# A pad of 160 bytes for 32 at the right end of SBUF, in a transformer block on one core

## The chip, the core and the metric

The kernel runs on one core of a Trainium2 chip. The time is that of the device for one execution, in microseconds. Before the change it is 955.4 us, the median of three runs (954.83 to 955.71).

The engines are called as in the profile: PE (TensorE, with PEld for its weight loads), DVE (VectorE), ACT (ScalarE), POOL (GpSimd), and SP, whose queue issues nearly all DMAs.

## The reference: what is computed

One transformer block over S = 2048 tokens of D = 512, in float32, with adaptive layer norms, sliding-window attention (32 heads of 16, window 256) and a SwiGLU feed-forward part (F = 1792):

```python
mod = (_silu(c) @ w_mod).reshape(c.shape[0], 6, 1, -1)
sa, ca, ga, sb, cb, gb = (mod[:, 0], mod[:, 1], mod[:, 2], mod[:, 3], mod[:, 4], mod[:, 5])
h = _layernorm(x, axis=-1) * (1 + ca) + sa
x = x + ga * _A_ref(h, A_wqkv, A_wo)        # qkv, masked softmax per head, output projection
h = _layernorm(x, axis=-1) * (1 + cb) + sb
x = x + gb * _B_ref(h, B_w1, B_w3, B_w2)    # (silu(h w1) * (h w3)) w2
```

## The kernel before, in words

**Precision.** Most products are made of two-part numbers: an operand is cut into a high part (an ACT copy to fp32r) and a low part (the rest, by DVE or POOL), and a product is three matmuls, high by high, high by low, low by high. One such matmul has a weight tile of 128x128, loaded before it, and a moving operand of 128x512. Every matmul loads other weights than the one ahead of it, so PE's rows alternate: a weight load, a matmul, a weight load, a matmul. In the trace the load for the next matmul starts a few ns after the current matmul does, so that the two read SBUF side by side.

**Stages.**
- Ahead of about 100 us: layer norm, the values' projection (`value`, L705: weights are 128-column slices of `hT`, the moving operand is `wvh` or `wvl`), and the first query and key projections.
- About 100 to 470 us, attention, in 32 units (8 groups of 4 heads by 4 blocks of tokens): the projection of queries and keys (`product`, L520: weights `wq`, moving `hT`), scores for the row maxima (L576) and for the probabilities (L933), both with weights and moving operand from the tile `ring` and moving 384 columns in the main, and the product with the values (L894: weights `vS`, moving `pt`).
- About 470 to 520 us: the output projection (`o_proj`, L1317: weights `o` or `x1b`, moving `wo`).
- From about 520 us: the feed-forward part, 14 rounds (2 halves of the tokens by 7 pairs of columns of F). In each round `ffn` makes the gate and the up product, each as 7 block products of 6 matmuls (`product`, L1581: weights `w` or, in every second round, `wo` and `o`; moving `b`). The results are combined on DVE, POOL and ACT, cut into two parts, and multiplied down (`down`, L1675: 8 blocks of 6 matmuls; weights are the slices of the cut results, moving `w2`).

The names `wo` and `o` stand for two things: the output projection's weights and inputs, and later the feed-forward weights of every second round (`second_open` puts those into the same places). The cut results of a round lie in `wq00`, `wq10`, `wq01`, `wq11`, `qkr`, `qk0`, `qk1`, `qk2`; in the last round four of the eight are `e0`, `e1`, `e2` and `wqr` instead.

**Order.** The order of instructions on every engine comes from a planner in the kernel with costs and offsets written out as tables. It knows nothing of addresses.

**Places in SBUF.** Pools are stacked from both ends of each partition's 224 KB: `cst`, `ap`, `p0`, `a2`, `fp` from the left, and `edge`, `a1`, `hp` (later `xp`) from the right. `edge` is the first pool on the right and holds one tile that nothing reads or writes. Everything on the right lies below it, so its size sets where all of them start:

```python
ctx.enter_context(tc.tile_pool(name="edge", bufs=1, side="right")).tile([P, 8], F32, name="edge")
a1 = ctx.enter_context(tc.tile_pool(name="a1", bufs=1, side="right", reuse_waits="tile"))
...
hp = hx.enter_context(tc.tile_pool(name="hp", bufs=1, side="right", reuse_waits="tile"))
hT = hp.tile([P, 2, KC, S], F32R, name="hT")
```

The start of the larger tiles in a partition, as the built programs have it, in bytes modulo 512 (a weight slice of 128 columns is 512 bytes, so all slices of a tile start at the same place modulo 512; a moving operand of 512 columns is 2048 bytes):

| side | tiles | before | after |
|---|---|---|---|
| left | `ring`, `vS`, `mskq`; feed-forward: `b`, `w` (all four tiles), `w2`, `t`, `g`, `e` | 448 | 448 |
| left | `wvh`, `wvl`; `pt`, `sm`, `jb`, `os` | 64 | 64 |
| left | `xt`, `h32` | 416 | 416 |
| right | `hT`; `x1a`, `x1b`, `wo`, `o`; `qkr`, `qk0`, `qk1`, `qk2`, `wqr`, `wq00`, `wq01`, `wq10`, `wq11` | 64 | 448 |
| right | `junk` (two buffers) | 128, 384 | 0, 256 |

Of the kernel before, what the change touches and what calls it, by code (L numbers as in the profile page):

```python
# [8 lines left out]
F32 = mybir.dt.float32  # L9
# [9 lines left out]
P = 128  # L19
# [349 lines left out]
def block_kernel(ctx: ExitStack, tc: tile.TileContext, x, wqk, wv, wo, w13, w2, c, crow, wmod, wmodt, out):  # L369
# [40 lines left out]

    psA = ctx.enter_context(tc.tile_pool(name="psA", bufs=1, space=PSUM))

    ctx.enter_context(tc.tile_pool(name="edge", bufs=1, side="right")).tile([P, 8], F32, name="edge")
    a1 = ctx.enter_context(tc.tile_pool(name="a1", bufs=1, side="right", reuse_waits="tile"))

    def ps(b):
# [1395 lines left out]
```

## Time and profile before

| | |
|---|---|
| median of 3 runs | 955.4 us (954.83 to 955.71) |
| the profiled execution | 954.43 us, of which its span from the first to the last instruction is 952.7 us |
| PE | 936.7 us busy (98%), 5296 matmuls |
| DVE / ACT / POOL | 734.2 (77%) / 560.8 (59%) / 497.6 us (52%) |
| granted TensorE clock, mean | 0.998 |
| DMA | 141.64 MB, 149 GB/s mean |
| chain that ended last | PE 86%, POOL 4%, DVE 4%, DMA 2%, ACT 2% |

A matmul's duration in the trace reaches to the modelled end of its pipeline, so consecutive matmuls overlap and durations can't be added up. The pace of PE is read from starts: in the chain that ended last, each piece runs from its start to the start of the next.

### The profile page before, as it was taken

The numbers are of one execution on the slowest core, as the hardware profiler recorded it, in microseconds if no ns is written. First come the engines' busy times: TensorE is split into PE (matmuls) and PEld (weight loads), VectorE is DVE, ScalarE is ACT, GpSimd is POOL, SyncE is SP. The second block draws the span as 40 slices with busy tenths as digits, with TensorE's granted clock in tenths as the row PEclk, the third lists the DMA queues.
The fourth block names the chain that finished last, engine by engine and source line by source line (L and its number), as shares of the span: only waits on it lengthen the run. The fifth ranks groups of instructions, "written<-read, shape, count | busy, mean of one in ns | idle before, by whom it ended". The sixth has DMA issues, their size and how long they took to land.

```text
span 952.7 us, 17091 instructions
## 1 busy us (share of the span) xinstructions
PE 936.7 (98%) x5296; PEld 715.5 (75%) x5296; DVE 734.2 (77%) x2065; ACT 560.8 (59%) x1263; POOL 497.6 (52%) x721
## 2 busy tenths in 40 slices
PE   8999999999999999998999999999999999999998
PEld 4678777777767677775688888888888888888886
DVE  7884989898989898989469775666689766667555
ACT  6443878787878787876779933433456333433230
POOL 3220877787777777767544655444866222221320
PEclk9999999999999999999999999999999999999999
DMA  8621454444544444436993555466684421322002
GB/s 310 209 68 37 127 185 146 147 146 147 160 166 146 146 147 146 136 129 207 261 275 100 175 160 200 136 187 215 223 287 144 149 79 60 99 83 78 23 23 88
DMA packets 81561, 141.64 MB, mean 149 GB/s; under 512 B 10555, under 2 KB 23227, under 8 KB 81470
## 3 DMA queue, kind: packets, MB, share of 16 engines
q1 hardware_dynamic: 81180, 140.29, 45.8%
q8 instruction: 42, 0.69, 0.3%
q14 instruction: 49, 0.40, 0.1%
q10 hardware_dynamic: 290, 0.27, 0.1%
HBM read 85.73 MB, written 34.61 MB: 126 GB/s over the span
## 4 chain that ended last, share of the span: by engine, by line
PE 86%; POOL 4%; DVE 4%; DMA 2%; ACT 2%; issue 2%; SPq 1%; POOLq 0%; DVEq 0%; ACTq 0%
PE st L1581 12%; PE mx L1581 10%; PE pj L520 8%; PE mx L576 7%; PE st L933 7%; PE mx L1675 7%; PE po L894 7%; PE st L1675 5%; PE pj L1581 3%; PE po L1581 3%; PE mx L705 2%; PE po L1675 2%; PE st L1317 2%; PE pj L1675 2%; PE mx L1317 2%; PE st L705 2%
## 5 line engine op out<-in xcount | busy, mean ns | idle before, releaser
L583 DVE CUSTOM_DVE_ANT_0 junk<-mx,mskq 128x384 bf16<-128x384 f32 (+1 forms) x482 | 242.1, 528 | 24.6 <-PE mx L576 23.2
L576 PE MATMUL mx<-ring 96*128 96x384 f32 (+2 forms) x482 | 144.8, 340 | 2.2 <-ACT pt L945 1.0
L933 PE MATMUL st<-ring 100*128 100x384 f32 (+2 forms) x484 | 145.7, 342 | 0.7 <-ACT pt L954 0.4
L961 POOL TENSOR_SCALAR_AFFINE_SELECT pt<-pt 128x256 f32<-128x256 f32 x268 | 108.1, 406 | 50.2 <-ACT pt L954 39.7
L520 PE MATMUL pj<-hT,wq 128*128 128x512 f32 x384 | 132.0, 403 | 0.0
L954 ACT ACTIVATE pt<-st 128x256 f32<-128x256 f32 x255 | 91.3, 386 | 36.1 <-DVE st L951 28.2
L576 PEld LDWEIGHTS mx<-ring 96*128 96x128 f32 x482 | 88.0, 189 | 31.5 <-DVE mt L583 21.1
L933 PEld LDWEIGHTS st<-ring 100*128 100x128 f32 x484 | 89.9, 189 | 18.9 <-issue 6.7
L1625 POOL TENSOR_TENSOR t<-t,t 128x512 f32<-128x512 f32 x28 | 41.6, 1485 | 113.8 <-DVE t L1613 106.7
L894 PE MATMUL po<-pt,vS 128*17 128x256 f32 (+2 forms) x1408 | 97.1, 387 | 2.4 <-ACT os L1001 1.0
L538 POOL TENSOR_TENSOR qk<-qkr,qk 128x512 fp32r<-128x512 f32 x64 | 82.8, 1293 | 10.2 <-ACT qkr L526 8.7
L1172 POOL TENSOR_TENSOR w<-w,w 128x512 fp32r<-128x512 f32 (+2 forms) x35 | 51.4, 1480 | 58.7 <-ACT w L1171 58.7
L1613 DVE TENSOR_TENSOR t<-st,t 128x512 f32<-128x512 f32 x55 | 37.8, 690 | 50.8 <-PE st L1581 38.3
L520 PEld LDWEIGHTS pj<-hT,wq 128*128 128x128 f32 x384 | 71.2, 189 | 7.5 <-issue 0.9
L951 DVE COPY_PREDICATED st<-later,st 128x128 f32<-128x128 uint8 x255 | 68.8, 291 | 7.6 <-PE st L933 4.4
L894 PEld LDWEIGHTS po<-pt,vS 128*17 128x17 f32 x1408 | 32.1, 96 | 48.4 <-issue 19.6
L1581 PE MATMUL st<-b,w 128*128 128x512 f32 x234 | 58.9, 390 | 0.0
L945 ACT ACTIVATE pt<-st 128x384 f32<-128x384 f32 (+2 forms) x113 | 47.0, 432 | 14.9 <-DVE st L941 13.7
L978 POOL TENSOR_SCALAR_AFFINE_SELECT sm<-sm 128x256 f32<-128x256 f32 x109 | 41.9, 406 | 24.2 <-ACT sm L968 21.4
L1581 PE MATMUL mx<-b,w 128*128 128x512 f32 x204 | 51.5, 390 | 0.0
L1581 PEld LDWEIGHTS st<-b,w 128*128 128x128 f32 x234 | 43.9, 188 | 9.3
L1653 ACT ACTIVATE qkr<-g 128x512 fp32r<-128x512 f32 x13 | 8.2, 632 | 66.5 <-DVE g L1609 66.5
(349 smaller groups left out, 2140.3 us busy)
## 6 DMA issues: line engine op xcount, KB each, us to landing
ring<-qk SPq DMA_DIRECT2D x192, 128.0 KB
o_dr<-os SPq DMA_DIRECT2D x32, 256.0 KB
w<-wsum SPq DMA_DIRECT2D x14, 512.0 KB
w<-w2g SPq DMA_DIRECT2D x14, 512.0 KB
jb<-in_w SPq DMA_DIRECT2D x24, 256.0 KB
vS<-in_wmodt SPq DMA_DIRECT2D x22, 256.0 KB
wraw<-in_w SPq DMA_DIRECT2D x7, 768.0 KB
w<-wraw SPq DMA_DIRECT2D x14, 384.0 KB
```

The source lines that it names most:

```text
L520: nc.tensor.matmul(v["ps"], WQ[g][w][:, n // 3], hTp(i, n // 3, b * BT, BT), start=(n == 0), stop=(n == 3 * KC - 1))
L538: nc.gpsimd.tensor_tensor(out=v[n], in0=v["raw"], in1=v[1].bitcast(F32), op=ALU.subtract)
L576: nc.tensor.matmul(v[i][:, :n], queries(NS, a, gq, 1), keys(NS, hh, a, k0, gq + 1 - k0), start=True, stop=True)
L583: nc.vector.tensor_tensor_reduce(out=junk[:, :n], in0=v[i][:, :n], in1=mskq[:, 3 * P - n:], scale=1.0, scalar=-3e38, op0=ALU.add, op1=ALU. ...
L894: nc.tensor.matmul(po[32 * i:32 * i + DH + 1, qb * P:(qb + nq) * P], vS[:, kb, 4 * g + i], pts[i // 2][:, i % 2, c0:c0 + nq], start=first, ...
L933: nc.tensor.matmul(ps[:, :nq], keys(NM, hh, a, kb, 1), queries(NM, a, kb, nq), start=True, stop=not plus)
L951: nc.vector.copy_predicated(ps[:, 0], later, ps[:, 2])
L954: nc.scalar.activation(pt_of(j, a)[:, hh, :2], v[j, a, hh][:, :2], AF.Exp, scale=SCALE)
L961: nc.gpsimd.affine_select(out=pt[:, :, 2 * m], in_=pt[:, :, 0], **w)
L1172: sch.op(eng, lambda: on_eng(eng).tensor_tensor(out=lo(), in0=src(), in1=hi().bitcast(F32), op=ALU.subtract), tt(eng, n), key, kl + kh, kl ...
L1581: nc.tensor.matmul(ps(bk), WT[s, n][w][:, col], BB[t, k][r], start=start and c == 0, stop=stop and c == 5, skip_group_check=True)
L1675: nc.tensor.matmul(ps(bk), tiles[hk + (h,)][:, i * P:(i + 1) * P], w2_of(last, y, f), start=(m == 0), stop=(m == 5))
```

## The change

The tile of the pool `edge` has 40 floats per partition where it had 8, that is 160 bytes for 32. Every tile on the right side moves down by 128 bytes. The left side stays. No instruction is added or removed, and on every engine the instructions stand in the same order with the same waits; only addresses of right-hand operands differ.

```diff
     psA = ctx.enter_context(tc.tile_pool(name="psA", bufs=1, space=PSUM))
 
-    ctx.enter_context(tc.tile_pool(name="edge", bufs=1, side="right")).tile([P, 8], F32, name="edge")
+    ctx.enter_context(tc.tile_pool(name="edge", bufs=1, side="right")).tile([P, 40], F32, name="edge")
     a1 = ctx.enter_context(tc.tile_pool(name="a1", bufs=1, side="right", reuse_waits="tile"))
```

## The prediction

> **What bounds the kernel now.** The page comes first: its busy times, and the chain that ended last by engine.
>
> ```profile
> span 952.7 us, 17091 instructions
> PE 936.7 (98%) x5296; PEld 715.5 (75%) x5296; DVE 734.2 (77%) x2065; ACT 560.8 (59%) x1263; POOL 497.6 (52%) x721
> PE 86%; POOL 4%; DVE 4%; DMA 2%; ACT 2%; issue 2%; SPq 1%; POOLq 0%; DVEq 0%; ACTq 0%
> ```
>
> PE carries the chain. The change touches no instruction, so it can act only where an address sets how long something takes. The place to look is PE's pace, and the second view is the chain in order of time inside the feed-forward part (start, length until the next piece starts, piece). I took 655 to 720 us, since there whole rounds of both kinds stand side by side.
>
> ```profile
> 662.86 2.79 PE mx L1581 x12
> ...
> 678.20 2.78 PE mx L1675 x12
> 680.98 2.79 PE st L1675 x12
> 683.77 1.40 PE pj L1581 x6
> ...
> 694.90 1.36 PE pj L1581 x6
> ...
> 707.14 1.36 PE st L1581 x6
> 708.50 1.37 PE mx L1581 x6
> ```
>
> Two paces are in it. From 662.86 to 678.20 stand 66 matmuls in 15.34 us, 232.4 ns each. From 678.20 to 683.77 stand 24 in 5.57 us, 232.1 ns each. From 694.90 to 708.50 stand 60 in 13.60 us, 226.7 ns each. The form is the same (128x128 weights, 512 columns). The third view, PE's timeline of the same stretch, says what differs:
>
> ```profile
> 662.69 2.96 PE L1581 MATMUL mx<-b,wo 128*128 128x512 f32 x12
> 678.50 1.09 PE L1675 MATMUL mx<-w,qk 128*128 128x512 f32 x4
> 694.74 1.52 PE L1581 MATMUL pj<-b,w 128*128 128x512 f32 x6
> ```
>
> In the slow rows the moving operand lies on the left at byte 448 modulo 512 (`b`, `w2`) and the weights on the right at 64 (`wo`, `o`, `qkr`, `qk`, `wq`). In the fast row both lie at 448. The stages view of exactly these two stretches keeps other causes out:
>
> ```profile
> 662.86:678.20 15.34, 15.34 (x67) 1.00 0.69 226
> 694.90:708.50 13.60, 13.60 (x61) 1.00 0.74 246
> ```
>
> PE is busy throughout both, the granted clock (behind the count) is 1.00 in both, and the DMA share is higher in the fast one. So neither waits, nor the clock, nor DMA traffic makes the slow pace.
>
> Is it the distance modulo 512, or that the weights are on the right? Two other stages tell. Their pieces of the chain, and two groups that name their operands (shortest, median and longest duration behind the count):
>
> ```profile
> 86.87 4.12 PE st L705 x18
> 91.00 2.04 PE mx L705 x9
> ```
>
> ```profile
> 475.34 2.72 PE mx L1317 x12
> 482.82 4.08 PE mx L1317 x18
> ```
>
> ```profile
> L705 PE MATMUL mx<-wvh,hT x72: 388/389/500, 21.4 to 92.6; 128*128 128x512 f32 x72
> L1317 PE MATMUL mx<-wo,o x48: 389/389/396, 475.2 to 518.5; 128*128 128x512 f32 x48
> ```
>
> In the values' projection (L705) the moving `wvh` is on the left and the weights, slices of `hT`, are on the right, both at 64: 2.04 us for 9 is 226.7 ns. In the output projection (L1317) both are on the right at 64: 4.08 us for 18 is 226.7 ns again. So right-hand weights run at the fast pace, with a moving operand from the left too, wherever both stand at the same byte modulo 512. I read the extra 5.7 ns (232.4 less 226.7) as the price of reading a moving operand and the next weights at different bytes modulo 512.
>
> The Trainium skill, in TensorE: Matmul & The Clock Gate, section "Step-by-step: what each phase is for", says that PE has two independent read ports and that loading the next weights takes no read bandwidth from the running matmul. By that rule alone the change would be worth nothing; the trace disagrees, with 232.4 against 226.7 ns for one form.
>
> **The change part by part.** *Feed-forward part.* After the change the right side is at 448 as well, so every pair of moving operand and weights in it meets at the same byte. How many matmuls are slow now: 7 of the 14 rounds have their gate and up weights in `wo` and `o`, each with 2 times 7 products of 6 matmuls, which is 588. The down products are 14 times 8 blocks of 6, 672, with right-hand weights in all but 20 (in the last round, for the second half of its blocks, five of six matmuls use `e0` to `e2`). That is 652. Together 1240 times 5.7 ns is 7.1 us.
>
> Do they lie on the path? In the stages view PE is busy for all of 530 to 930 us:
>
> ```profile
> 530.00:930.00 400.00, 400.00 (x1750) 1.00 0.43 137
> ```
>
> What would be late next if PE goes faster: a slow round (84 matmuls at L1581, 48 at L1675) becomes shorter by 0.75 us of some 30, the others by about 0.27. The engines that feed and empty PE wait there themselves (waits from 530 to 950 us: total, times, longest):
>
> ```profile
> POOL w L1172 <- ACT w L1171: 57.9, 14, 14.3
> DVE t L1613 <- PE st L1581: 38.3, 34, 2.1
> ```
>
> DVE waits for PE's results and POOL has up to 14 us to spare in cutting weights, so I count nothing back; if this cover were thin, I allow up to 2 us lost over the 14 rounds. The term is 7.1 us less, between 5.0 and 8.2 less (the upper end takes the slowest of the quoted pieces, 1.40 us for 6, which is 233.3 ns and 6.6 over the fast pace).
>
> *Values' projection.* `hT` moves to 448 and `wvh`, `wvl` stay at 64, so its 192 matmuls lose their match: at 5.7 ns, 1.1 us more. How much is on the path, by the chain's shares of the first 100 us:
>
> ```profile
> by line: PE mx L705 22.9%; PE st L705 14.9%; PE pj L520 8.8%; PE po L766 6.0%; DVE vS L723 5.8%; PE st L732 3.8%; PE st L576 3.1%; DVE hT L699 3.1%; PE st L685 3.1%; PE mx L576 2.7%; PE mx L685 2.7%; PE mx L732 2.7%; issue 2.4%; DVE xt L676
> ```
>
> 37.8 us of the 43.5 (192 times 226.7 ns) are on it, so the bound is 0.95 us. The distance here is 384 bytes where the feed-forward part has 128, and no fast-form row shows 384 by itself; the lower bound is nothing. I take 0.8 us more, nearer to the row that shows a price.
>
> *Attention.* Here `hT` and `wq` (64, later 448) alternate with `ring` (448), so matches are gained: behind a projection step the next weights are often of `ring`, and the other way round. But the timeline shows little to gain:
>
> ```profile
> 65.33 2.01 PE L520 MATMUL pj<-hT,wq 128*128 128x512 f32 x8
> 67.18 0.34 PE L576 MATMUL st<-ring 96*128 96x384 f32 x1
> ...
> 265.43 0.86 PE L520 MATMUL pj<-hT,wq 128*128 128x512 f32 x3
> 266.13 0.34 PE L933 MATMUL st<-ring 100*128 100x384 f32 x1
> 266.31 0.34 PE L576 MATMUL mx<-ring 96*128 96x384 f32 x1
> 266.48 0.34 PE L933 MATMUL st<-ring 100*128 100x384 f32 x1
> 266.66 0.40 PE L520 MATMUL pj<-hT,wq 128*128 128x512 f32 x1
> 266.90 0.34 PE L933 MATMUL st<-ring 100*128 100x384 f32 x1
> ```
>
> Three projection steps in a row (both operands at 64) take 0.70 us, 233 ns each, and one with `ring` behind it 240 ns; eight in a row take 1.85 us, 231 ns. Scores followed by scores take 0.17 to 0.18 us, scores followed by a projection 0.18 us. So in this mix even the matched steps are slow. Perhaps a mismatch is felt for a step or two, and in runs this short the fast pace is never reached; after the change the runs of matched steps become longer. The bound: 384 projection steps and 848 score steps of 384 columns, in these groups,
>
> ```profile
> L933 PE MATMUL st<-ring 100*128 100x384 f32 x424 | 132.7, 352 | 0.7 <-ACT pt L954 0.4 <-ACT pt L945 0.2
> L520 PE MATMUL pj<-hT,wq 128*128 128x512 f32 x384 | 132.0, 403 | 0.0
> L576 PE MATMUL mx<-ring 96*128 96x384 f32 x424 | 131.3, 349 | 2.2 <-ACT pt L945 1.0 <-DVE st L951 0.7 <-ACT pt L954 0.4
> ```
>
> each 2 ns faster (233 to 231, the step of the longest run), is 2.5 us less. A loss is possible too where `pt` (64) now meets `wq` at 448, but that is one step per unit, under 0.2 us over 32 units. I take 0.5 us less, nearer to the rows in which match and mismatch read alike.
>
> *Other engines.* DVE, ACT, POOL and the DMA queues get new addresses as well. In the feed-forward rounds the work of ACT, DVE and POOL already goes both from left to left (448 to 448) and from left to right (448 to 64), without a wait that PE's rows would show; I cost it at nothing.
>
> **The sum.** 7.1 less, 0.8 more, 0.5 less: 6.8 us less. The span goes from 952.7 to 945.9 us. The profiled execution took 954.43 us, 1.73 more than its span, so it would be 947.6; the median of the runs, 955.4, is 1.0 above that execution, which gives 948.6 us.
>
> **The rivals.**
>
> *No match is needed; right-hand weights are slow for another reason (the same time, 955.4 us).* All slow rows of the feed-forward part do have their weights on the right. Against it stand L705 and L1317, with right-hand weights at 226.7 ns. Chance 0.05.
>
> *The match at 448 is paid for elsewhere.* Once the right side stands at 448 too, ACT and DVE write the cut results there while PE reads at 448, and half of the steps might stay slow: 3.5 us less in place of 7.1, hence 952.2 us. Against it: in the fast rounds PE reads at 448 while `t` and `g` at 448 are read and written, at 226.7 ns. Chance 0.05.
>
> *A denser PE loses clock (slower).* The feed-forward part is 420 us of PE without a break. If the faster pace drew a lower granted clock there, each per cent would cost 4.2 us; from 1.7% on the gain is gone, and at 3% the time is 955.4 less 6.8 plus 12.6, 961.2 us. For it: the matmul array would work 2.5% more densely in the slow stretches. Against it: the granted clock reads 1.00 in 13.6 us at the fast pace and over 530 to 930 us, which holds both. Chance 0.04.
>
> **How the numbers follow.** The forecast has 0.86, with 948.6 us. Its low end is 8.2 and 2.5 less, nothing lost in the values' projection, and 0.5 for the spread of the runs: 944.2, which I draw in to 945.0, since these ends are unlikely together. Its high end is 5.0 less, 0.95 more, and nothing gained in attention: 951.4, drawn in to 951.2 for the same reason. The rivals lie outside, with 0.14. A measurement of this kernel can tell about 0.2%, 1.9 us, from no change. Faster by more than that are the forecast and the second rival, 0.91; within it the first, 0.05; slower the third, 0.04.
>
> **What would show it.** Right: the chain after shows 1.36 us for 6 at L1581 and L1675 in every round, whatever the operands; the feed-forward part, from the first L1581 to the last L1675, is about 7 us shorter; L705 pieces of 9 take 2.09 us in place of 2.04. Wrong: rows with `b,wo` or `w,qk` still at 1.40 us for 6 (the first rival), both kinds at some 1.38 (the second), a granted clock below 0.99 between 530 and 930 us (the third), or an attention stage that moves by more than 2.5 us.

## The result, and the profile after

The changed kernel takes 947.3 us, the median of four runs (946.36 to 948.02), against 955.1 us before (four runs, 953.89 to 955.71): a ratio of 0.992, 95% interval 0.990 to 0.994. The profiled execution took 948.02 us, its span is 946.3 us.

The page after, span and busy times:

```profile
span 946.3 us, 17091 instructions
PE 930.7 (98%) x5296; PEld 716.4 (76%) x5296; DVE 736.4 (78%) x2065; ACT 560.1 (59%) x1263; POOL 498.0 (53%) x721
```

PE is busy 6.0 us less with the same 5296 matmuls; DVE, ACT and POOL work as long as before, to within 2.2 us. The chain in order of time, in the stretch where the prediction read two paces:

```profile
661.93 2.72 PE mx L1581 x12
664.65 2.72 PE st L1581 x12
...
676.89 2.72 PE mx L1675 x12
679.61 2.72 PE st L1675 x12
682.33 1.36 PE pj L1581 x6
...
693.21 1.36 PE pj L1581 x6
```

One pace is left: 1.36 us for 6, in rounds with `wo` and `o`, in rounds with `w`, and in the down products. The 66 steps of the round with `wo` and `o`, from its first piece to the first down product, take 14.96 us where they took 15.34, 226.7 ns each. The stages view of 530 to 900 us says the same by counting, before and then after (length, PE busy and matmuls, PEld, DVE, ACT and POOL likewise, granted clock, DMA):

```profile
530.00:900.00 370.00, 370.00 (x1621) 302.22 (x1620) 256.50 (x336) 159.39 (x251) 159.95 (x145) 1.00 0.46 147
```

```profile
530.00:900.00 370.00, 370.00 (x1651) 306.87 (x1650) 262.22 (x344) 160.29 (x253) 160.59 (x145) 1.00 0.45 147
```

PE is busy without a break in both, at clock 1.00, and gets through 30 matmuls more. The length of the whole feed-forward part is read from the start of its first matmul to the start of its last one (the first and the last start of a group stand behind its durations), before and then after:

```profile
L1581 PE MATMUL st<-b,w x234: 388/389/396, 513.3 to 903.5; 128*128 128x512 f32 x117
L1675 PE MATMUL mx<-w,wq x144: 390/393/404, 561.3 to 948.1; 128*128 128x512 f32 x144
```

```profile
L1581 PE MATMUL st<-b,w x234: 388/389/397, 514.6 to 898.2; 128*128 128x512 f32 x117
L1675 PE MATMUL mx<-w,wq x144: 388/389/389, 562.1 to 941.7; 128*128 128x512 f32 x144
```

From 513.3 to 948.1 it was 434.8 us, from 514.6 to 941.7 it is 427.1: 7.7 us less. It begins 1.3 us later, however. The product with the values marks attention, before and after:

```profile
L894 PE MATMUL po<-pt,vS x1408: 271/379/499, 98.8 to 470.5; 128*17 128x384 f32 x64, 128*17 128x256 f32 x56, 128*17 128x128 f32 x56
```

```profile
L894 PE MATMUL po<-pt,vS x1408: 271/379/847, 99.2 to 471.8; 128*17 128x384 f32 x64, 128*17 128x256 f32 x56, 128*17 128x128 f32 x56
```

0.4 us were lost ahead of attention and 0.9 in it (371.7 us before, 372.6 after). The loss in attention goes with a lower clock, not with the change: in this execution the granted clock fell to 0.70 from 445 to 450 us and to 0.62 from 450 to 455 us, behind a wait for the DMA that brings `wo` from `wog` (439.27 us, 6.49 us long), and the stages view has a mean of 0.93 around it. In the changed kernel's second profile (below) the clock stayed at 1.00 there, and attention took 371.9. Four of the kernels below whose addresses in attention are those of before show such a fall too. Why it comes in some executions is not known; the kernel before has the same wait, 6.38 us, at a clock of 1.00.

```profile
430.00:480.00 50.00, 46.10 (x321) 0.93 0.77 229
```

### The profile page after: what moved, and what is told of

It is laid out like the page before. It is cut to its first block, busy times and chain, and to the rows that moved or that the text cites. A ratio compares the mean times of both kernels' runs of the same rounds, so it can differ in the third digit from the quotient of the medians.

```text
span 946.3 us, 17091 instructions
## 1 busy us (share of the span) xinstructions
PE 930.7 (98%) x5296; PEld 716.4 (76%) x5296; DVE 736.4 (78%) x2065; ACT 560.1 (59%) x1263; POOL 498.0 (53%) x721
## 4 chain that ended last, share of the span: by engine, by line
PE 86%; DVE 4%; POOL 4%; ACT 2%; DMA 2%; issue 2%; SPq 0%; POOLq 0%; DVEq 0%; ACTq 0%
PE st L1581 12%; PE mx L1581 10%; PE pj L520 8%; PE mx L576 7%; PE st L933 7%; PE po L894 7%; PE mx L1675 7%; PE st L1675 5%; PE pj L1581 3%; PE po L1581 3%; PE po L1675 2%; PE mx L705 2%; PE st L1317 2%; PE pj L1675 2%; PE mx L1317 2%
```

## The experiments

Theory 1 says that a matmul step is slow where moving operand and weights stand at different bytes modulo 512. Theory 2 says that it is the place or the side: that the right side is better off at 448 than at 64. All pads below hold nothing and move only what lies behind them.

**The changed kernel again** is the measure for the three that follow, on the same chip, with the kernel before at 954.1 us. The later ones ran on other chips, each with the kernel before beside it, so their ratios are what to compare.

> The changed kernel once more, beside the kernel before on the same chip, as the measure for the others. 0.992 of the kernel before (947.3 where that is 955.1), with 1.36 us for 6 matmuls at L1581 and L1675 in every round and 2.10 us for 9 at L705.

It took 947.2 us, ratio 0.993 (0.992 to 0.994).

**A pad on the left instead of the right.**

```diff
             pools["fp"] = fp
+            fp.tile([P, 32], F32, name="fedge")
```

> The pad on the right stays at 32 bytes; instead the pool fp on the left begins with 128 unused bytes, so that in the feed-forward part both sides meet at byte 64. Theory 1 (what counts is that moving operand and weights stand at the same byte modulo 512, wherever that is): all of L1581 and L1675 at 1.36 us for 6, 7.1 to 7.7 us less; L705 stays at 2.04 us for 9 and attention as before, so 947.5 us or, without the 0.8 us that the values' projection cost in the changed kernel, down to 946.5. Theory 2 (the right side is better off at 448 than at 64): no change, 955.1.

946.6 us, ratio 0.992 (0.991 to 0.994). The chain, in the feed-forward part and at the end of the values' projection:

```profile
662.39 2.72 PE mx L1582 x12
...
677.35 2.72 PE mx L1676 x12
...
693.67 1.36 PE pj L1582 x6
```

```profile
84.57 2.04 PE mx L705 x9
```

Every row is fast although the right side stands at 64 as before. Theory 2 has fallen: it is not the side and not the place, but where the two operands stand to each other.

**The values' projection matched as well.** In the changed kernel the small tiles of `p0` go first, with 32 bytes behind them, so that `wvh` and `wvl` come to 448.

```diff
+    mv = p0.tile([P, NT, 2], F32, name="mv")
+    rs = p0.tile([P, NB, 2, 4], F32, name="rs")
+    bst = p0.tile([P, 4, nc.vector.BN_STATS_DIM], F32, name="bst")
+    p0.tile([P, 8], F32, name="pedge")
     crep = p0.tile([P, D], F32, name="crep")
 ...
-    mv = p0.tile([P, NT, 2], F32, name="mv")
-    rs = p0.tile([P, NB, 2, 4], F32, name="rs")
-    bst = p0.tile([P, 4, nc.vector.BN_STATS_DIM], F32, name="bst")
```

> The changed kernel, with the small tiles of the pool p0 ahead of crep, wvh and wvl and 32 unused bytes behind them, so that wvh and wvl stand at 448 as hT does. Theory 1: L705 back at 2.04 us for 9, 0.8 to 1.0 us less than the changed kernel, 946.4; if attention gains from hT and wq standing at 448 as ring does, this kernel is ahead of the one with the pad on the left by that gain (the forecast took 0.5, at most 2.5 us). Theory 2: nothing to gain at L705, 947.3.

The same pieces of the chain, in the changed kernel's first profile and here:

```profile
87.26 4.18 PE st L705 x18
91.44 2.10 PE mx L705 x9
```

```profile
86.22 4.12 PE st L706 x18
90.34 2.04 PE mx L706 x9
```

The pace of these pieces is as expected: 2.10 us for 9 where `hT` and `wvh` stand apart, 2.04 where they match. The time is 946.8 us, ratio 0.992 (0.991 to 0.993), against the 947.2 of the changed kernel: with these intervals the gain of the 0.8 us is not shown, nor is a lead over the pad on the left.

**Only the pool `xp` moved**, so that `wo` and `o` meet `b` at 448 and the down products stay mismatched.

```diff
         hx.close()
+        ctx.enter_context(tc.tile_pool(name="xedge", bufs=1, side="right")).tile([P, 32], F32, name="xedge")
```

> The pad stays at 32 bytes; 128 unused bytes stand above the pool xp alone, so that only wo, o, x1a and x1b move to 448, and the weights of the down product (pool a1) and hT stay at 64. Theory 1: the 588 slow matmuls of L1581 become fast, 3.4 us less (951.7), L1675 stays at 1.40 us for 6 and L705 at 2.04 for 9. If the gain were one of the whole stage (fewer collisions with what DVE and ACT write there), L1675 would move too, or less than 3.4 us would come.

951.7 us, ratio 0.998 (0.997 to 0.999); between the starts of the first and the last matmul the feed-forward part takes 432.3 us, 2.5 less than before, not 3.4. The chain where the two kinds alternate and where they don't:

```profile
682.19 1.38 PE pj L1582 x6
683.57 1.40 PE mx L1676 x6
684.97 1.37 PE po L1582 x6
...
690.50 1.40 PE st L1676 x6
691.90 1.39 PE st L1582 x6
693.29 1.36 PE pj L1582 x6
```

L1676 (the down product) stays at 1.40. L1582 is at 1.36, but at 1.37 to 1.39 just behind a down product. That less than 3.4 us came was named as a sign that the gain is one of the whole stage. Against that reading stand the down products, which gained nothing: by the starts of single matmuls in the trace (a step is the time from one start to the next), the 588 steps with `wo` and `o` became 2.8 us shorter (3.4 in the changed kernel), and all the others 0.4 longer. Of the 0.5 us by which the steps with `wo` and `o` gained less than in the changed kernel, nearly all stands in the first six steps behind a down product. So the gains of the two parts don't add up: matched steps next to mismatched ones are slow too. That was put to a test of its own.

**Only the low parts of `w` off.** In the changed kernel, every third matmul of the rounds with `w` is mismatched.

```diff
-                WT[0, n] = [fp.tile([P, 7 * PH], F32R, name=f"w{n}{part}") for part in range(2)]
+                WT[0, n] = [fp.tile([P, 7 * PH], F32R, name=f"w{n}0")]
+                fp.tile([P, 32], F32, name=f"wa{n}")
+                WT[0, n].append(fp.tile([P, 7 * PH], F32R, name=f"w{n}1"))
+                fp.tile([P, 96], F32, name=f"wb{n}")
```

> The changed kernel (everything in the feed-forward part at 448), but the low parts of the weights w on the left stand at 64, so that in the 7 rounds with w every third matmul (low part of the weights) meets its moving operand at another byte. If a mismatch costs its own step alone: 196 steps of 5.7 ns, 1.1 us more than the changed kernel, and a mean of 228.6 ns at L1581 with w. If it is felt in the steps behind it too: all 588 steps slow, 3.4 us more, a mean of 232 ns, though two thirds of them match.

949.1 us, ratio 0.994 (0.993 to 0.996); feed-forward part 429.6 us, 2.5 more than the changed kernel, between the two expectations. The chain of a round with `w`:

```profile
691.43 1.39 PE st L1584 x6
692.82 1.39 PE pj L1584 x6
...
706.68 1.39 PE mx L1584 x6
708.07 1.36 PE pj L1678 x6
```

72 steps in 16.64 us are 231.1 ns. By the starts of single matmuls the three steps of a triple take 232 to 233, 234 and 227 ns. The first is the step beside which the mismatched weights are loaded, the second the step that uses them. So one mismatch costs two steps, some 13 ns, and the third step is at the full pace again; 196 times 13 ns is the 2.5 us that were found. In an unbroken run of mismatches each step pays 5.7 (the kernel before).

**Only `b` moved.**

```diff
             pools["fp"] = fp
+            fp.tile([P, 32], F32, name="fedge")
 ...
+            fp.tile([P, 96], F32, name="wedge")
             for n in range(2):
                 WT[0, n] = [fp.tile([P, 7 * PH], F32R, name=f"w{n}{part}") for part in range(2)]
```

> The pad on the right stays at 32 bytes (right side at 64); of the pool fp on the left the moving tiles b alone move to 64, w, w2 and the rest stay at 448. Theory 1 (distance modulo 512): the kinds of round change places. Those with weights w on the same side as b become slow (232 ns a step), those with wo and o on the other side fast (226.7 ns, next to the slow down products a little more), the down products stay at 232; the time is about that of the kernel before, within 2 us. Theory 2 (weights on the right, or operands on two sides, are what is slow): no row changes its pace.

954.0 us, ratio 1.000 (0.999 to 1.001). The kinds have changed places, as theory 1 has it:

```profile
666.27 2.73 PE mx L1583 x12
...
681.25 2.79 PE mx L1677 x12
...
697.94 1.40 PE pj L1583 x6
```

From 666.27 the weights are `wo` and `o` at 64, on the other side of SBUF, and fast; from 696.54 they are `w`, next to `b` on the left, and slow. There `w` stands 384 bytes past `b` modulo 512, and 66 steps take 15.40 us, 233.3 ns each, where the 128 bytes of the kernel before give 232.4.

**Other distances.** The pad at the head of `fp` was made 384, 96, 64 and 448 bytes (`[P, 96]`, `[P, 24]`, `[P, 16]` and `[P, 112]` in the diff of the pad on the left), so that the weights on the right stand 256, 32, 64 and 192 bytes (modulo 512) past the moving operands.

> The pad on the right stays at 32 bytes; the pool fp begins with 384 unused bytes, so that its tiles stand at 320 and the right side at 64: a distance of 256 in place of 128. If the rule goes by bytes modulo 512: still slow, some 232 ns a step in rounds with wo and o and in the down products, 954 us. If it goes modulo 256: fast everywhere, 226.7 ns and about 946.6 us.

> The pad on the right stays at 32 bytes; the pool fp begins with 96 unused bytes, so that its tiles stand at 32 and the right side at 64: a distance of 32 bytes, 8 of the 512 columns. If any other byte costs the whole price: 232 ns a step and 954 us. If the price grows with the distance, a quarter of it at 32 against 128: 228 ns a step, about 948.5 us.

> After a distance of 256 was as fast as 0 and a distance of 32 as slow as 128: the pool fp begins with 64 unused bytes (its tiles at 0, the right side at 64), a distance of 64. If only the same byte modulo 256 is fast: some 232 ns a step in rounds with wo and o and in the down products, 954 us. If the slow distances are those that share no 64-byte row (the period is 64 and 128 is slow for another reason): fast, about 946.6 us.

> The pool fp begins with 448 unused bytes (its tiles at 384, the right side at 64): a distance of 192 modulo 256, the last multiple of 64 not yet tried. Same byte modulo 256 alone fast: 954 us and some 232 ns a step. Fast if the law has another period: about 946.6 us.

The first piece of a round with `wo` and `o`, and the first of the down products behind its 66 steps, for 256, 32, 64 and 192 in turn:

```profile
659.13 2.72 PE mx L1582 x12
...
674.09 2.72 PE mx L1676 x12
```

```profile
665.65 2.80 PE mx L1582 x12
...
681.05 2.80 PE mx L1676 x12
```

```profile
664.51 2.80 PE mx L1582 x12
...
679.91 2.80 PE mx L1676 x12
```

```profile
660.39 2.75 PE mx L1582 x12
...
675.50 2.75 PE mx L1676 x12
```

| weights past the moving operand, bytes modulo 512 | 66 steps, us | one step, ns | ratio to the kernel before (95%) |
|---|---|---|---|
| 0 (the change) | 14.96 | 226.7 | 0.992 (0.990 to 0.994) |
| 32 | 15.40 | 233.3 | 1.001 (0.9995 to 1.002) |
| 64 | 15.40 | 233.3 | 1.002 (1.001 to 1.004) |
| 128 (before) | 15.34 | 232.4 | 1 |
| 192 | 15.11 | 228.9 | 0.995 (0.993 to 0.997) |
| 256 | 14.96 | 226.7 | 0.992 (0.990 to 0.995) |

A distance of 256 is as good as none, 192 costs 2.2 ns a step, and 32, 64 and 128 cost 5.7 to 6.6. So theory 1 holds with a period of 256 bytes, not 512, as far as these distances go: 384, which is 128 modulo 256, is slow as 128 is (above). The price is not the same for every mismatch, and it is not symmetric: 192, which is 64 short of a period, costs a third of what 64 costs. Nor does the distance alone set it. With `b` alone moved the down products still stand 128 apart; by single starts, in the 30 of them from 713.2 us two steps in turn take 229 to 230 and 237 to 238 ns, some 233.3 in the mean, while the 30 from 744.9 us soon repeat the seven steps of the kernel before (228 to 241 ns, 232.4 in the mean). One distance gives both paces; what picks between them is not known.

No version is shown to beat the change: those with a match all through the feed-forward part lie at 0.992 or 0.993, within each other's intervals.

## Why the prediction was right, point by point

**Feed-forward part: right, a little low.** The term was 7.1 us, the part became 7.7 us shorter (427.1 for 434.8), inside the stated 5.0 to 8.2. By the starts of single matmuls, the 588 steps with `wo` and `o` gave 3.4 us, as counted, the down products 3.9 where 3.7 were counted, and the steps with `w`, counted at nothing, 0.4, nearly all of it next to down products. That is the effect that the kernel with only the low parts off shows: a mismatch slows the neighbouring step too, so that matched steps beside the down products had been slow as well and gained. POOL and DVE keep their waits (below, the waits after from 530 to 945 us, as before total, times, longest), and PE is busy without a break, so the faster PE met nothing late.

```profile
POOL w L1172 <- ACT w L1171: 56.5, 14, 14.0
DVE t L1613 <- PE st L1581: 35.2, 33, 2.0
```

**Distance, not side: right, the period was wrong.** The kernels with the pad on the left and with `b` alone moved show it. "Modulo 512" went further than the rows could: before, only distances of 0 and 128 could be read in the feed-forward part, and both 256 and 512 fit them. That this did no harm to the forecast is luck: the change uses only distances (0, 128, 384) on which the two periods agree. The 256 bytes were found by trying. The Trainium skill, in TensorE: Matmul & The Clock Gate, section "Step-by-step: what each phase is for", has loading the next weights take no read bandwidth from the running matmul. The runs agree with that only where the distance is 0 or 256 (226.7 ns), and measure up to 233.3 elsewhere; the measurement decides. By what mechanism the distance acts, no run shows.

**Values' projection: the pace of unbroken rows right, the price too high.** L705 went to 2.10 us for 9, against 2.09 foreseen. But the 1.1 us from which the term came takes all 192 steps as fast before, and they were not. Behind a wait or a step with other operands, matched steps are slow as well for a while: the piece of 18 from 86.87 us, which the prediction shows, took 4.12 us, 228.9 ns each, and by single starts nine of its steps take 224 to 236 ns before the 226 to 227 set in. By single starts again, without those above 245 ns, a step took 229.1 to 229.7 ns in the eight profiles with `hT` and `wvh` both at 64, 231.9 to 232.2 in the three with `hT` alone at 448, and 229.0 with both at 448. So the term that was mis-sized is the price per step: some 2.7 ns, 0.5 us for 192 steps, where 5.7 ns and 0.8 us on the path were taken. The start of attention can't show as little: it came at 99.2 and 99.0 us in the changed kernel's two profiles (below, the second), and between 97.6 and 99.1 in the eight profiles in which nothing ahead of it was moved.

```profile
L894 PE MATMUL po<-pt,vS x1408: 271/379/498, 99.0 to 470.9; 128*17 128x384 f32 x64, 128*17 128x256 f32 x56, 128*17 128x128 f32 x56
```

**Attention: no gain that the stage shows.** 0.5 us less was taken. In the changed kernel's second profile, where the clock stays up, attention takes 371.9 us against 371.7. The timeline there has all of `hT`, `wq` and `ring` at 448, and still:

```profile
266.17 0.85 PE L520 MATMUL pj<-hT,wq 128*128 128x512 f32 x3
266.86 0.34 PE L933 MATMUL st<-ring 100*128 100x384 f32 x1
267.04 0.34 PE L576 MATMUL mx<-ring 96*128 96x384 f32 x1
267.21 0.34 PE L933 MATMUL st<-ring 100*128 100x384 f32 x1
```

Three projection steps take 0.69 us, 230 ns each, score steps 0.17 to 0.18 as before. By single starts from 105 to 430 us, without those of 300 ns and more, a projection step took 235.1 to 235.9 ns in the eight profiles with `hT` and `wq` at 64 and 234.3 to 234.7 in the four with them at 448; the score steps did not move (181.9 to 182.4 in all). About 0.9 ns for 384 steps is 0.4 us, an estimate close to the 0.5. The length of the stage can't show it: at a clock of 1.00, attention took 370.5 to 371.9 us in four profiles with the right side at 64, and 371.0 to 372.2 in three with it at 448.

So a match helps these steps a little, but it is not the mismatch that mainly slows them: the matches came, and they are still far from 226.7. That in runs this short the fast pace is never reached, as the prediction guessed, fits what L705 shows behind a break, since from 105 to 430 us the projection steps stand alone or in threes. Why matched steps need a run of several to reach the fast pace stays open.

**The sum and the rivals.** 6.8 us less was forecast, 948.6 us; 7.8 less was measured, 947.3 (the other 0.3 us between the two times is the kernel before, 955.4 in the forecast and 955.1 beside the changed kernel). The feed-forward term was 0.6 us too small and the loss in the values' projection, by the estimate above, 0.3 too large; both make the forecast too small, and the 0.1 by which attention's gain was too large goes the other way. What is left of the 1.0 us is well inside the spread of the runs, 946.4 to 948.0. The first rival (right-hand weights slow for another reason) is refuted by the pad on the left. The second (the match paid for by DVE's and ACT's accesses at 448) did not come: no row stays slow. The third (a denser PE loses clock) did not come either, since the granted clock is 1.00 from 530 to 900 us at the faster pace.

## What to carry to other kernels

Where matmuls follow each other with a weight load each and PE is the bound, compare their start-to-start times by operand names: two paces of one form with the same clock and no waits can come from addresses, as here. Then put moving operands and weights at the same byte modulo 256 with a pad, and check the pairs that the pad pulls apart, here the values' projection. What it is worth is about the number of mismatched steps on the path times the difference of the two paces. An alternation of matched and mismatched steps pays for its matched ones too, and where short runs are broken by waits or other operands, matched steps are slow anyway and a match is worth less: 2.7 ns a step in the values' projection, 0.9 in attention, 5.7 in the unbroken rows.

## What the runs showed of the hardware that was not expected

- The period of the effect is 256 bytes in the runs made: a distance of 256 gives 226.7 ns a step as 0 does.
- The price depends on the distance: 6.6 ns at 32 and 64 bytes, 2.2 at 192, and at 128 (modulo 256) 5.7 in the kernel before and 5.7 or 6.6, from row to row, with `b` alone moved.
- One mismatched weight load in three steps slows two steps, to 232 to 233 and 234 ns, and the third runs at 227.
- A mean pace hides a pattern: in unbroken mismatched runs of the kernel before, the single steps go from 228 to 241 ns and repeat every 7, and with 32 or 64 bytes they alternate between 230 to 232 and 235 to 236. In unbroken matched runs of the kernel before and the changed one they are all 226 or 227.
- Behind a break, matched steps are slow too for up to some ten steps (224 to 236 ns at L705 behind 86.9 us in the kernel before).
